# One load per attention-output unit and per output-weight piece, with rows ordered by head first and the value columns permuted

## The chip, the core and the metric

The kernel runs on one core of a Trainium2 chip. The metric is the device time of one execution in microseconds (us). Engines are named as the profile names them: PE (TensorE matmul), PEld (its weight load), DVE (VectorE), ACT (ScalarE), POOL (GpSimd) and SP (SyncE, which issues nearly all DMAs here). Before the change, the median of three runs is 849.85 us (848.42 to 851.2).

## What is computed

One layer: a normalized input goes through sliding-window attention (32 heads of width 20, window 256) and through a squared-relu MLP, and the attention is gated by the silu of the MLP.

```python
# S, D, F, H, Dh, W = 2048, 640, 1536, 32, 20, 256
xn = layernorm(x)
q, k, v = split_heads(xn @ wqkv)                  # 3 x 32 heads x 2048 x 20
scores = where(0 <= i - j < W, q @ k.T * Dh ** -0.5, -1e9)
s = concat_heads(softmax(scores) @ v) @ wo        # 640 x 640
r = relu(xn @ w1 + b1)
g = silu((r * r) @ w2 + b2)
out = x + s * g
```

All tensors are float32. The kernel splits an operand of a matmul into a rounded high part and a low rest, and takes three products (high by high, high by low, low by high).

## The kernel before

**Stages.** First (up to about 118 us) the input is normalized and transposed, the value weights `wv` are split, and the value products `vps` and the first query and key columns are made. Then follows one long loop of steps over head pairs and 128-row tiles; a step has score matmuls (`sps`, `stps`), the exponentials and, every few steps, a burst of value products (`ops`). Between them a filler puts matmuls of the remaining query/key columns (`qkps`), the MLP's first (`hps`) and second (`yps`) layer, and at the very end the output product (`wops`). PE's order is fixed when the program is built, and PE is in order.

**Order by a planner's clock.** Pieces that evacuate, split or fetch are put off by `later(wait, fn)`: they are emitted when a planned clock, advanced by the matmuls' planned costs, passes the due time. `BRING` is such a wait: the first unit's normalization, `turn_out(0, ...)`, comes `BRING` after its load was emitted.

**Value weights.** `load_w`/`wvr` bring five chunks of 128 rows of the value columns. `split_w` makes the high part on ACT (L188, `wv<-wvr`) and the rest on POOL (L189). The products `vps` (L233) for the first two row tiles take all high parts first (20 matmuls), then the five low parts, a chunk at a time.

**Attention output.** Each pair of heads, 512 rows of the sequence, and their sums of exponentials lie in a DRAM scratch `o_d[g]` as `[16 pairs, 128, 256]`: the 128 rows of a pair are four blocks of 32, by head and by parity of the row tile, of which 20 are the head's values and the next is its sum. A *unit* `u` (eight of them) is one parity of one `g`. `load(u)` brings it to `ob`, partitions `32 k + head`, chunk `c` holding value row `4 c + k` of the head: four DMAs of 32 partitions each (L1126), each with 5 runs of 256 numbers a partition. A fifth DMA (L1127) brings the inverted sums to `sums`. `turn_out(u, 0)` multiplies `ob` by `sums` on DVE (L1145, two pieces) and rounds it on ACT (L1146); `turn_out(u, 1)` makes the rests on DVE (L1149, two pieces). The output product (L627) of a unit contracts those 128 partitions, chunk by chunk, with five pieces of `wo` whose rows lie in the same order: each is four DMAs of 32 rows (L800) into `raw`, then a high part on ACT (L825) and a rest on DVE (L826).

**MLP output.** Each half row of `yps` (18 matmuls in each half of the array) is accumulated in one of three PSUM banks and evacuated by one DVE instruction, `ysb` (L1013). PE's next `yps` group in that bank waits for it.

**DMA queue.** SP issues in program order. Completion is counted on eight semaphores (`DMAHW0` to `DMAHW7` in the order of instructions) taken in turn, and a DMA waits until the one that had its semaphore before, eight earlier, is complete.

Of the kernel before, what the change touches and what calls it, by code (L numbers as in the profile page):

```python
# [19 lines left out]
H = 32  # L20
DH = 20
# [5 lines left out]
VW = DH + 1  # L27
# [7 lines left out]
MT = 256  # L35
# [14 lines left out]
SETTLE = 0.45  # L50
LEAD = 0.15
FETCH = 8.0
BRING = 8.0
SOON = 0.25
PATIENCE = 0.5

# [1 line left out]
def f32(ap):  # L58
    return ap.bitcast(F32)
# [3 lines left out]
def attn_mlp_kernel(ctx: ExitStack, tc, x, wqkv, wo, w1, b1, w2, b2, out):  # L63
    nc = tc.nc
# [25 lines left out]
    o_d = [dram.tile([NP, P, MT], F32, name=f"o_{g}") for g in range(NB)]  # L90
# [47 lines left out]
    with tc.tile_pool(name="ph1v", bufs=2) as p1v, tc.tile_pool(name="ph1", bufs=2) as p1, tc.tile_pool(name="ph1x", bufs=4) as p1b, tc.tile_pool(name="ph1w", bufs=1) as p1w, tc.tile_pool(name="ph1t", bufs=2, space=PSUM) as p1t:  # L138
# [9 lines left out]
        wv = [p1w.tile([P, KC, D], F32R, name=f"wv{p}") for p in range(2)]  # L148
# [119 lines left out]
        with tc.manual_schedule(engines={E_.PE, E_.Activation, E_.DVE, E_.Pool, E_.SP}):  # L268
# [15 lines left out]
            wjobs = []  # L284
# [6 lines left out]
            wvr = [wvt[c // 3][:, c % 3 * D:(c % 3 + 1) * D] for c in range(KC)]  # L291
            for c in range(KC):
                nc.sync.dma_start(wvr[c], wqkv[c * P:(c + 1) * P, 2 * D:3 * D])
                wjobs.append((wv[0][:, c, :], wv[1][:, c, :], wvr[c]))

            def root(t):
                nc.scalar.activation(rstd[:, t:t + 1], mv[:, t, 1:2], AF.Sqrt, bias=eps)
# [195 lines left out]
    def max_rows(p, g, tps):  # L493
        i = p % 2

        def one(j):
            r = slice(j * HP, (j + 1) * HP)
            nc.tensor.transpose(tps[:HP, j, 3 * P:3 * P + HP], mts[g % 2][r, :], ident[r, r])
        both(lambda: one(0), lambda: one(1), COST[P])

        def rest():
            row = at2.tile([8, P], F32, tag="row", bufs=1, name="row")
            mrow = at2.tile([8, 2, P], F32R, tag="mrow", bufs=1, name="mrow")
            nc.scalar.activation(row.rearrange("m (j n) -> m j n", j=2), tps[:8, :, 3 * P:3 * P + HP], AF.Copy, scale=-1.0)  # L504
            nc.scalar.activation(mrow[:, 0, :], row, AF.Copy)
            nc.gpsimd.tensor_sub(mrow[:, 1, :], row, f32(mrow[:, 0, :]))
            for a in range(2):
                nc.sync.dma_start(f32(qs[i])[KR + a:KR + a + HP + 1:HP, g * BT:(g + 1) * BT].rearrange("h (q n) -> h q n", q=4), f32(mrow)[:, a, :])
        return rest
# [3 lines left out]
    def pair_tile():  # L513
        return ptp.tile([P, 2, BT], F32, tag="st", name="stps")
# [25 lines left out]
    def burst_at(p, kb):  # L540
        return next((ts for ts in bursts(p) if ts[-1] == kb), None)
# [57 lines left out]
    def later(wait, fn):  # L599
        tasks.append((clock[0] + wait, len(tasks), fn))  # L600
# [177 lines left out]
    def subtract(tag, jobs):  # L778
        left = [len(jobs)]

        def put_off(k, job):
            def go():
                if item in lows:
                    lows.remove(item)
                    job()
                    left[0] -= 1
                    if not left[0]:
                        held[0] -= 1
            item = (tag, go)
            lows.append(item)  # L790
            later(1.9 + 0.7 * k, go)
        for k, job in enumerate(jobs):
            put_off(k, job)

    def piece(tag, src, go):
        def start():
            raw = wgt.tile([P, FHALF], F32, tag="wraw", bufs=RAW, name="raw")[:, :RAWN[tag[0]]]
            if isinstance(src, list):
                for k, rows in enumerate(src):
                    nc.sync.dma_start(raw[32 * k:32 * k + H], rows)  # L800
                return lambda tag: go(tag, raw)
            if len(src.shape) == 3:
                raw = raw.rearrange("p (c n) -> p c n", n=src.shape[-1])
            nc.sync.dma_start(raw, src)
            return lambda tag: go(tag, raw)
        queue.append((tag, start))
# [16 lines left out]
    def piece_pair(tag, hi, lo, src):  # L823
        def go(tag, raw):
            nc.scalar.activation(hi(), raw, AF.Copy)  # L825
            subtract(tag, [lambda: nc.vector.tensor_sub(lo(), raw, f32(hi()))])  # L826
        piece(tag, src, go)

    def lazy(make):
        got = []  # L830

        def get():
            if not got:
                got.append(make())
            return got[0]
        return get
# [42 lines left out]
    def filler():  # L879
# [53 lines left out]
        def late():  # L933
            j = lates[0]
            lates[0] += 1
            if j >= 3:
                load(0)
            if j >= 5:
                load(1)
            if j >= 7:  # L940
                load(2)

        for n, (hf, b) in enumerate(blocks):
# [6 lines left out]
            if n == last:  # L950
                wo_part = queue_wo()
                shut.add("o")
# [116 lines left out]
    rec_d = [dram.tile([2, H, MT], F32, name=f"rec_{g}") for g in range(NB)]  # L1069
# [47 lines left out]
    def load(u):  # L1117
        if u in ld or u >= 2 * NB or recs.get(u // 2, 0) is not None:
            return
        if u % 2 == 0:  # L1120
            obs[u // 2] = bigp.tile([P, KC * BT], F32, tag="big", name=f"ob_{u // 2}")
        ob = obs[u // 2][:, u % 2 * 2 * D:(u % 2 + 1) * 2 * D].rearrange("p (c n) -> p c n", c=KC)
        sums = at2.tile([P, MT if u // 2 % 3 == 0 else BT], F32, tag=("sums", "relu", "sq")[u // 2 % 3], name="sums")[:, :MT]
        rows = o_d[u // 2].rearrange("p (h r) n -> (p h) r n", h=2)[:, 32 * (u % 2):32 * (u % 2) + VW]
        for k in range(4):
            nc.sync.dma_start(ob[32 * k:32 * k + H], rows[:, k:DH:4])  # L1126
        nc.sync.dma_start(sums, rec_d[u // 2][u % 2].unsqueeze(0).to_broadcast([4, H, MT]))  # L1127
        ld[u] = (ob, sums)
        if not u:
            for part in range(2):  # L1130
                later(BRING + 2.0 * part, lambda part=part: turn_out(0, part))

    obs, oT, turned_out, shone = {}, {}, set(), set()

    def turn_out(u, part):
        if (u, part) in turned_out or u not in ld:
            return
        turned_out.add((u, part))
        ob, sums = ld[u]
        cuts = (slice(0, 2), slice(2, KC))  # L1140
        if not part:
            big = bigp.tile([P, KC * BT], F32R, tag="big", name=f"oT_{u}")
            oT[u] = big.rearrange("p (s c n) -> p s c n", s=2, c=KC)
            for cs in cuts:
                nc.vector.tensor_mul(ob[:, cs], ob[:, cs], sums.unsqueeze(1).to_broadcast([P, cs.stop - cs.start, MT]))  # L1145
                nc.scalar.activation(oT[u][:, 0, cs], ob[:, cs], AF.Copy)  # L1146
        else:
            for cs in cuts:
                nc.vector.tensor_sub(oT[u][:, 1, cs], ob[:, cs], f32(oT[u][:, 0, cs]))  # L1149
            if whole[0]:  # L1150
                silu(u)
# [9 lines left out]
    def queue_wo():  # L1161
        wob = lazy(lambda: [bigp.tile([P, KC * BT], F32R, tag="big", name=f"wo{j}") for j in range(2)])
        wo4 = lazy(lambda: [wgt.tile([P, FHALF], F32R, tag="wraw", bufs=RAW, name=f"wo4{w}")[:, :D] for w in "hl"])

        def wo_part(p, c):
            return wob()[p][:, c * D:(c + 1) * D] if c < 4 else wo4()[p]

        for c in range(KC):
            piece_pair("o", lambda c=c: wo_part(0, c), lambda c=c: wo_part(1, c), [wo.rearrange("(h d) n -> d h n", d=DH)[4 * c + k] for k in range(4)])
        return wo_part  # L1170

    def out_filler(wo_part):
# [71 lines left out]
    with tc.manual_schedule(engines={E_.PE, E_.Activation, E_.DVE, E_.Pool, E_.SP}):  # L1244
# [7 lines left out]
        for s in range(steps):  # L1252
# [8 lines left out]
            if a:  # L1261
                p, q = a
# [12 lines left out]
            rows = None  # L1275
# [4 lines left out]
            if s % 4 == 0 and 0 < s <= NP * NT:  # L1280
                rows = max_rows((s - 1) // NT, (s - 1) % NT // 4, stp[0] if b else pair_tile())
# [11 lines left out]
            r = e and burst_at(*e)  # L1293
# [41 lines left out]
```

## Time and profile before

| | before |
|---|---|
| median of three runs | 849.85 us |
| the profiled execution, its own time | 851.8 us |
| its span, first to last instruction | 849.7 us |
| mean granted TensorE clock | 0.995 |
| moved by DMA | 166.42 MB, mean 196 GB/s |
| `ob<-o` | 32 DMAs of 160 KB |
| `raw<-in_A_wo_dram` | 20 DMAs of 80 KB |
| `sums<-rec` | 8 DMAs of 128 KB |

So 2.1 us of the profiled execution lie outside its span. In the profile's timeline a row gives the start, the duration, the engine, the line, the instruction and its output and inputs; brackets hold the idle time of the engine before it and what ended it. The windows view gives the busy time of each engine in a stretch, with the instruction count in brackets, then the granted clock (PEclk, 1.00 is full), the busy share of the 16 DMA engines and the rate that they moved. The waits view sums who waited for whom: total, times, longest. A busy PE is not the same as a PE at its peak, because ends of matmuls are modelled.

### The profile page before, as it was taken

Reading aid. Unit: us, or ns where it says so; the run is one execution under the profiler, and the core shown is the slowest. Engines: PE = TensorE matmul, PEld = TensorE weight load, DVE = VectorE, ACT = ScalarE, POOL = GpSimd, SP = SyncE. Lnnn points to the kernel's source line nnn. Section 1 sums busy time; section 2 is a strip of 40 time slices with the busy share of each in tenths; the row PEclk is TensorE's granted clock in tenths of the full one; section 3 lists DMA queues with packets and bytes.
Section 4 is the critical chain, followed back from the end, with each engine's and each line's share of the span. In section 5 each row is a group of like instructions: output and inputs, shape, how many; then the busy total and the mean of one; then the engine's idle time right before and its main releaser. Section 6 shows DMA issues by size and latency. Waiting matters only on the chain.

```text
span 849.7 us, 25547 instructions
## 1 busy us (share of the span) xinstructions
PE 836.9 (98%) x10176; PEld 787.0 (93%) x10176; DVE 458.6 (54%) x1370; ACT 420.5 (49%) x792; POOL 329.9 (39%) x652
## 2 busy tenths in 40 slices
PE   8999999999999999999999999999999999989997
PEld 8999999988888999999999999899999999979997
DVE  7643126666577645455455476654455455345653
ACT  5232104555566754754754765745745736742321
POOL 5010002434334543553543644534533634532443
PEclk9999999999999999999999999999999999999999
DMA  7998488879989555364365264485285374376994
GB/s 245 284 389 336 161 207 259 256 249 273 300 268 302 128 182 156 84 200 132 78 214 166 77 179 136 128 266 154 63 269 135 110 223 120 102 171 180 274 231 150
DMA packets 94398, 166.42 MB, mean 196 GB/s; under 512 B 10952, under 2 KB 43848, under 8 KB 93256
## 3 DMA queue, kind: packets, MB, share of 16 engines
q1 hardware_dynamic: 94120, 164.64, 64.4%
q8 instruction: 80, 1.31, 0.7%
q14 instruction: 38, 0.31, 0.1%
q10 hardware_dynamic: 160, 0.16, 0.1%
HBM read 93.66 MB, written 70.52 MB: 193 GB/s over the span
## 4 chain that ended last, share of the span: by engine, by line
PE 87%; DMA 6%; DVE 2%; issue 2%; ACT 1%; SPq 1%; POOL 0%; DVEq 0%; ACTq 0%; POOLq 0%
PE yps L473 20%; PE hps L473 19%; PE qkps L473 14%; PE ops L561 10%; PE vps L233 8%; PE stps L523 5%; PE sps L483 4%; DMA ob<-o 4%; PE qkps L210 3%; PE wops L627 2%; DMA sums<-rec 1%; DMA yk<-y 1%; PE tps L177 1%; DMA o<-osb 1%; SPq L1126 0%
## 5 line engine op out<-in xcount | busy, mean ns | idle before, releaser
L491 DVE CUSTOM_DVE_ANT_0 junk<-sps,mask 128x384 bf16<-128x384 f32 (+2 forms) x512 | 272.1, 532 | 257.8 <-PE sps L483 86.8
L529 ACT ACTIVATE p<-stps 128x768 f32<-128x768 f32 (+2 forms) x256 | 197.4, 771 | 248.3 <-PE stps L523 203.0
L530 POOL TENSOR_SCALAR_AFFINE_SELECT p<-p 128x256 f32<-128x256 f32 x256 | 109.9, 429 | 326.1 <-ACT p L529 318.2
L473 PE MATMUL yps<-w,hh 64*128 64x320 f32 x1536 | 228.5, 312 | 4.2 <-DVE ysb L1013 3.4
L473 PE MATMUL hps<-xb,w 64*128 64x256 f32 (+1 forms) x2100 | 211.9, 304 | 0.0
L473 PEld LDWEIGHTS hps<-xb,w 64*128 64x128 f32 x2100 | 194.5, 187 | 3.8 <-issue 2.7
L473 PEld LDWEIGHTS yps<-w,hh 64*128 64x128 f32 x1536 | 187.0, 187 | 7.8 <-DVE ysb L1013 4.4
L473 PE MATMUL yps<-w,hl 64*128 64x320 f32 x768 | 177.8, 311 | 0.0
L483 PE MATMUL sps<-ks,qs 60*128 60x384 f32 (+2 forms) x512 | 131.5, 335 | 0.6 <-DVE mt L491 0.5
L523 PE MATMUL stps<-qs,ks 62*128 62x384 f32 (+2 forms) x512 | 126.3, 333 | 0.3 <-ACT row L504 0.2
L473 PEld LDWEIGHTS yps<-w,hl 64*128 64x128 f32 x768 | 120.4, 187 | 1.1 <-issue 1.0
L473 PE MATMUL qkps<-xT,wgkh 64*128 64x512 f32 x320 | 100.5, 394 | 0.0
L473 PE MATMUL qkps<-xT,wgqh 64*128 64x512 f32 x320 | 98.6, 392 | 0.0
L532 POOL TENSOR_SCALAR_AFFINE_SELECT p<-p 128x256 f32<-128x256 f32 x224 | 95.9, 428 | 0.0
L561 PE MATMUL ops<-p,vp 128*21 128x128 f32 (+1 forms) x2128 | 86.9, 311 | 0.0
L483 PEld LDWEIGHTS sps<-ks,qs 60*128 60x128 f32 x512 | 81.9, 185 | 4.4 <-DVE mt L491 2.2
L561 PEld LDWEIGHTS ops<-p,vp 128*21 128x21 f32 x2128 | 63.8, 100 | 21.2 <-issue 6.1
L523 PEld LDWEIGHTS stps<-qs,ks 62*128 62x128 f32 x512 | 80.7, 187 | 1.2 <-ACT row L504 0.6
L233 PE MATMUL vps<-wv,xT 128*128 128x320 f32 x480 | 71.5, 308 | 0.0
L233 PEld LDWEIGHTS vps<-wv,xT 128*128 128x128 f32 x480 | 70.5, 188 | 0.1
L983 POOL TENSOR_TENSOR hl<-sq,hh 128x512 fp32r<-128x512 f32 x48 | 62.2, 1295 | 16.4 <-ACT sq L982 16.2
L627 PE MATMUL wops<-wo,oT 128*128 128x320 f32 x384 | 62.2, 310 | 0.2 <-DVE res L1209 0.2
(104 smaller groups left out, 1160.1 us busy)
## 6 DMA issues: line engine op xcount, KB each, us to landing
ks<-k_d SPq DMA_DIRECT2D x64, 240.0 KB
qs<-q_d SPq DMA_DIRECT2D x64, 240.0 KB
xb<-xs SPq DMA_DIRECT2D x60, 256.0 KB
xs<-xT SPq DMA_DIRECT2D x8, 1280.0 KB
k_d<-shm SPq DMA_DIRECT2D x19, 512.0 KB
q_d<-shm SPq DMA_DIRECT2D x19, 512.0 KB
y<-ysb SPq DMA_DIRECT2D x28, 320.0 KB
o<-osb SPq DMA_DIRECT2D x64, 128.0 KB
```

What stands on the lines that cost most here:

```text
L210: nc.tensor.matmul(ps, wt[:, c, :], xT[part][b][:, c * BT + t0:c * BT + t0 + n], start=m == 1, stop=m == 3 * KC)
L233: nc.tensor.matmul(ps, xT[xp][b][:, c * BT + t * P: c * BT + (t + 1) * P], wv[wp][:, c, nh * HALF:(nh + 1) * HALF], start=first and m == 0 ...
L473: return nc.tensor.matmul(out, a[r], b_[r], skip_group_check=True, **kw)
L483: nc.tensor.matmul(ss[hh][:, :nk], qs[i][o, q * P:(q + 1) * P], ks[i][o, k0 * P:k0 * P + nk], start=True, stop=True)
L491: nc.vector.tensor_tensor_reduce(out=junk[:, :nk], in0=ss[hh][:, :nk], in1=mask[:, 3 * P - nk:], scale=1.0, scalar=-3.0e38, op0=ALU.add, o ...
L523: nc.tensor.matmul(tps[:, hh, :n], ks[i][o, kb * P:(kb + 1) * P], qs[i][o, kb * P:kb * P + n], start=True, stop=True)
L529: nc.scalar.activation(p32[:, :, :n], tps[:, :, :n], AF.Exp, scale=SCALE)
L530: nc.gpsimd.affine_select(p32[:, :, 0:P], p32[:, :, 0:P], pattern=[[0, 2], [1, P]], compare_op=ALU.is_ge, fill=0.0, base=0, channel_multip ...
L532: nc.gpsimd.affine_select(p32[:, :, 2 * P:], p32[:, :, 2 * P:], pattern=[[0, 2], [-1, P]], compare_op=ALU.is_gt, fill=0.0, base=0, channel ...
L561: nc.tensor.matmul(ot[r0:r0 + VW, c0:c0 + len(part), :], vps[p][:, kb // 4, kb % 4, hh, :], pt[:, hh, :].rearrange("p (t n) -> p t n", n=P ...
L627: nc.tensor.matmul(ps, a, b_, start=j == 0, stop=j == n - 1)
L983: nc.gpsimd.tensor_sub(hh[1][:, :BT], sq, f32(hh[0]))
```

## The change

The unit's rows are ordered by head first: `ob`'s partition is now `4 head + k`, and chunk `c` of it holds row `5 k + c` of the head in the scratch. So the five rows of a partition are one run of 1280 numbers, and the whole unit is one DMA of 128 partitions; `sums` is broadcast in the same order. For chunk `c`, partition `4 head + k` still to meet `wo` row `4 c + k` of the head, the 20 value columns of each head are permuted where `wv` is split: the split reads column `4 c + k` and writes column `5 k + c`. A `wo` piece is then the four rows `4 c` to `4 c + 3` of each head, one DMA of 128 partitions. `BRING` goes from 8 to 9.

```diff
-BRING = 8.0
+BRING = 9.0
...
-                wjobs.append((wv[0][:, c, :], wv[1][:, c, :], wvr[c]))
+                wjobs.append((*(w[:, c, :].rearrange("p (h k c) -> p h k c", h=H, k=4) for w in wv), wvr[c].rearrange("p (h c k) -> p h k c", h=H, k=4)))
...
-            if isinstance(src, list):
-                for k, rows in enumerate(src):
-                    nc.sync.dma_start(raw[32 * k:32 * k + H], rows)
+            if tag[0] == "o":
+                nc.sync.dma_start(raw, src)
                 return lambda tag: go(tag, raw)
...
-        rows = o_d[u // 2].rearrange("p (h r) n -> (p h) r n", h=2)[:, 32 * (u % 2):32 * (u % 2) + VW]
-        for k in range(4):
-            nc.sync.dma_start(ob[32 * k:32 * k + H], rows[:, k:DH:4])
-        nc.sync.dma_start(sums, rec_d[u // 2][u % 2].unsqueeze(0).to_broadcast([4, H, MT]))
+        rows = o_d[u // 2].rearrange("p (h r) n -> (p h) r n", h=2)[:, 32 * (u % 2):32 * (u % 2) + DH]
+        nc.sync.dma_start(ob.rearrange("p c n -> p (c n)"), rows.rearrange("h (k c) n -> h k (c n)", k=4))
+        nc.sync.dma_start(sums, rec_d[u // 2][u % 2].unsqueeze(1).to_broadcast([H, 4, MT]))
...
-            piece_pair("o", lambda c=c: wo_part(0, c), lambda c=c: wo_part(1, c), [wo.rearrange("(h d) n -> d h n", d=DH)[4 * c + k] for k in range(4)])
+            piece_pair("o", lambda c=c: wo_part(0, c), lambda c=c: wo_part(1, c), wo.rearrange("(h d) n -> h d n", d=DH)[:, 4 * c:4 * c + 4])
```

The order of PE's and POOL's instructions is the same in both programs. On DVE it differs in one place, at the first unit's normalization, just after the last `wo` piece. Before:

```order
L826 TENSOR_TENSOR wo4l<-raw,wo4h 128x640
L1084 RECIPROCAL rec<-rec 128x128
L1145 TENSOR_TENSOR ob_13901<-ob_13901,sums 128x512
L1145 TENSOR_TENSOR ob_13901<-ob_13901,sums 128x768
L1013 TENSOR_TENSOR ysb<-yps,yin 128x320
L1149 TENSOR_TENSOR oT_14055<-ob_13901,oT_14055 128x512
L1149 TENSOR_TENSOR oT_14055<-ob_13901,oT_14055 128x768
```

and now, at the same place of DVE's program:

```order
L825 TENSOR_TENSOR wo4l<-raw,wo4h 128x640
L1083 RECIPROCAL rec<-rec 128x128
L1012 TENSOR_TENSOR ysb<-yps,yin 128x320
L1143 TENSOR_TENSOR ob_13886<-ob_13886,sums 128x512
L1143 TENSOR_TENSOR ob_13886<-ob_13886,sums 128x768
L1147 TENSOR_TENSOR oT_14059<-ob_13886,oT_14059 128x512
L1147 TENSOR_TENSOR oT_14059<-ob_13886,oT_14059 128x768
```

The evacuation `ysb` has moved ahead of the two multiplications of `ob` (new lines are one or two lower in number). On ACT the last exponential, 128x2x128, likewise moves ahead of the first unit's two roundings.

On SP the queue before, from the load of the first units on (`o_85` to `o_88` are the four scratches `o_d`, `rec` the sums on their way through DVE):

```order
L1081 DMA rec<-o_86 64x1x128 x2
L1126 DMA ob_13901<-o_85 32x5x256 x4
L1127 DMA sums<-rec_1359 128x1x256
L1126 DMA ob_13901<-o_85 32x5x256 x4
L1127 DMA sums<-rec_1359 128x1x256
L930 DMA yin<-y_83 128x640
L1085 DMA rec_1360<-rec 128x128
L588 DMA o_87<-osb 128x256
L1081 DMA rec<-o_87 64x1x128 x2
L1126 DMA ob_14103<-o_86 32x5x256 x4
```

and now, from the same place:

```order
L1080 DMA rec<-o_86 64x1x128 x2
L1124 DMA ob_13886<-o_85 128x1x1280
L1125 DMA sums<-rec_1359 128x1x256
L1124 DMA ob_13886<-o_85 128x1x1280
L1125 DMA sums<-rec_1359 128x1x256
L929 DMA yin<-y_83 128x640
L1084 DMA rec_1360<-rec 128x128
L588 DMA o_87<-osb 128x256
L1080 DMA rec<-o_87 64x1x128 x2
L1124 DMA ob_14080<-o_86 128x1x1280
```

Where four loads stood, one stands; the order of the others is unchanged.

## The prediction

> **What bounds the kernel now.** I read the page's head first, then PE's waits, then the chain of waits around the longest one.
>
> ```profile
> span 849.7 us, 25547 instructions
> PE 836.9 (98%) x10176; PEld 787.0 (93%) x10176; DVE 458.6 (54%) x1370; ACT 420.5 (49%) x792; POOL 329.9 (39%) x652
> ```
>
> PE is busy for 836.9 of 849.7 us and its order does not change, so the time can fall only where PE waits or runs at a lower clock, and rise only where a new wait appears. PE's waits, and those of its weight loads, have one large entry:
>
> ```profile
> PE yps L473 <- DVE ysb L1013: 3.4, 1, 3.4
> PEld yps L473 <- DVE ysb L1013: 4.4, 4, 3.7
> ```
>
> One single wait of 3.7 us on the evacuation `ysb`. The chain of waits shows why it was late (start, duration, what):
>
> ```profile
> 748.49 2.05 PE yps L473 x28
> ...
> 756.50 4.22 DMA ob<-o
> 760.73 0.11 DVE ob L1145
> 761.32 0.95 DVE ob L1145
> 762.27 0.41 DVE ysb L1013
> 762.73 5.18 PE yps L473 x35
> ```
>
> and DVE's timeline at that place:
>
> ```profile
> 754.02 0.95 DVE L1084 RECIPROCAL rec<-rec 128x128 f32<-128x128 f32 x1
> 760.71 1.56 DVE L1145 TENSOR_TENSOR ob<-ob,sums 128x512 f32<-128x512 f32 x2 [5.74 <-DMA ob<-o]
> 762.19 0.48 DVE L1013 TENSOR_TENSOR ysb<-yps,yin 128x320 f32<-128x320 f32 x1
> 762.59 1.55 DVE L1149 TENSOR_TENSOR oT<-ob,oT 128x512 fp32r<-128x512 f32 x2
> 764.74 0.49 DVE L1013 TENSOR_TENSOR ysb<-yps,yin 128x320 f32<-128x320 f32 x1 [0.59 <-PE yps L473]
> ```
>
> DVE stood 5.74 us before the first `ob` multiplication, whose data was still landing. `ysb` is queued behind it, and PE wanted that PSUM bank. The wait has a second price, read in two windows:
>
> ```profile
> 757.00:763.00 6.00, 2.60 (x34) 2.34 (x32) 2.29 (x4) 1.33 (x2) 0.00 (x0) 0.91 0.97 187
> 763.00:775.00 12.00, 12.00 (x110) 11.21 (x111) 4.94 (x8) 4.81 (x9) 0.92 (x1) 0.76 0.59 151
> ```
>
> The third number from the end is the granted clock: 1.00 elsewhere, 0.91 and 0.76 here. PE came back slow: 35 matmuls took 5.18 us, 0.148 us each, against 2.05 us for 28, 0.073 each, just before the wait.
>
> **Part 1, the evacuation goes first.** In the new order `ysb` stands behind the reciprocal that ended at 754.97 and waits for its own matmuls and for a `yin` load, which SP issues ahead of the `ob` loads (749.07, below). It runs as soon as they end, before PE stops at about 759. This removes 3.7 us less one normal spacing, **3.6 us**, and the slow stretch, 5.18 - 35 x 0.073 = **2.6 us**. That doesn't hang on how fast the new load is, since `ob` no longer stands ahead of `ysb`.
>
> What is late next? After that wait PE begins only one more group with this bank rule; it goes on to the output product, which needs `oT`:
>
> ```profile
> 771.79 1.01 PE L627 MATMUL wops<-wo,oT 128*128 128x320 f32 x5
> 772.74 1.52 PE L561 MATMUL ops<-p,vp 128*21 128x128 f32 x40
> ```
>
> That start moves from 771.8 to 765.6. At the old landing, 760.7, multiplications and rests are done by 764.1 (the 762.59 row plus 1.55), so 1.5 us remain even with no faster load.
>
> **Part 2, the load itself.** SP's rows up to the first two units:
>
> ```profile
> 749.07 0.38 SPq L930 DMA_DIRECT2D yin<-y  x1
> ...
> 751.73 2.64 SPq L1126 DMA_DIRECT2D ob<-o  x4
> 754.41 0.58 SPq L1127 DMA_DIRECT2D sums<-rec  x1
> 755.03 1.91 SPq L1126 DMA_DIRECT2D ob<-o  x4
> ```
>
> Four issues become one, about 0.5 us instead of 1.9. The rate, from windows full of 32-partition `ob` loads and full of 128-partition loads of 2560 bytes a row (last number, GB/s):
>
> ```profile
> 754.00:759.00 5.00, 5.00 (x85) 4.61 (x78) 0.97 (x2) 0.87 (x2) 1.07 (x3) 1.00 1.04 216
> 789.00:793.00 4.00, 4.00 (x29) 4.00 (x29) 2.13 (x4) 0.47 (x1) 2.79 (x3) 1.00 1.05 408
> ```
>
> No row shows a 128-partition load with runs of 5120 bytes; between 216 and 408 I take 400, the row whose partitions are alike. A unit of 640 KB then takes 1.6 instead of 3.0 us. That matters at the end:
>
> ```profile
> 817.05 1.27 DVE L1209 TENSOR_TENSOR res<-wops,yk 128x320 f32<-128x320 f32 x3
> 822.48 1.56 DVE L1145 TENSOR_TENSOR ob<-ob,sums 128x512 f32<-128x512 f32 x2 [4.16 <-DMA ob<-o]
> ...
> 817.41 0.31 PE L627 MATMUL wops<-wo4h,oT 128*128 128x320 f32 x1
> 817.67 2.00 PE L627 MATMUL wops<-wo,oT 128*128 128x320 f32 x12
> ...
> 824.20 0.31 PE L627 MATMUL wops<-wo4h,oT 128*128 128x320 f32 x1
> 824.50 2.02 PE L627 MATMUL wops<-wo,oT 128*128 128x320 f32 x12
> ...
> 826.65 0.31 PE L627 MATMUL wops<-wo4h,oT 128*128 128x320 f32 x1
> 827.15 1.99 PE L627 MATMUL wops<-wo,oT 128*128 128x320 f32 x12 [0.19 <-DVE res L1209]
> ```
>
> DVE waits for loads there, and `wops` starts that normally follow at 0.147 us (1.76 for 12) come after 0.26, 0.30 and 0.50 us: 0.11 + 0.15 + 0.35 = **0.6 us** of PE. With six loads 1.4 us shorter each, 8.4 us of DMA time, I count all of it gone. The loads, stores and sums of the last stage follow PE by its evacuations, so they move 6.2 us earlier with it; the shorter loads are the cover for that. The single `wo` loads save SP issues under work that has slack (0 us), and the changed order of `sums` moves the same bytes (0 us).
>
> **Part 3, the permuted split at the start.** The POOL rests of `wv` now read `wvr` with a step of four numbers. ACT reads it so too.
>
> ```profile
> 15.27 7.68 POOL L189 TENSOR_TENSOR wv<-wvr,wv 128x640 fp32r<-128x640 f32 x5
> 20.27 8.96 PE L233 MATMUL vps<-wv,xT 128*128 128x320 f32 x60
> 15.29 1.99 ACT L188 ACTIVATE wv<-wvr 128x640 fp32r<-128x640 f32 x3
> 17.44 0.75 ACT L188 ACTIVATE wv<-wvr 128x640 fp32r<-128x640 f32 x1
> ```
>
> POOL goes through five rests of 1.54 us without a gap, to 22.95. PE starts at 20.27 and takes 0.149 us a matmul: after 20 high parts, at 23.25, it wants the five rests, the fifth at 23.85. Slack **0.9 us**: each rest may grow by 0.18 us for nothing, beyond that PE waits. ACT's last high part ends at 18.19 and is wanted at 20.27 + 8 x 0.149 = 21.46: 3.3 us over five pieces of 0.74, so it is covered unless they nearly double. The same values are made, so nothing later changes.
>
> No row shows a stepped read on POOL. The nearest are two fills of 64 numbers, with a step and without:
>
> ```profile
> L241 POOL MEMSET vt<- 128x64 f32 x8 | 1.8, 241 | 42.8 <-DMA v_d<-vt 42.8
> L104 POOL MEMSET mt<- 128x64 f32 x2 | 0.2, 151 | 0.0
> ```
>
> The stepped one costs 90 ns more, 1.4 ns a number; times 640 that is 0.9 us a rest. Ends: nothing, or 5 x 0.9 - 0.9 = 3.6 us of PE. The fill writes and the rest reads, so I take the middle, 0.54 us a rest: 2.7 - 0.9 = **1.8 us**, all on the fifth piece.
>
> [...]
>
> **Sum.** -3.6 - 2.6 - 0.6 + 1.8 = -5.0 us. The profiled execution, 851.8 us with 2.1 outside its span, would become 846.8. It lies 1.95 above the median, and on the median's scale the forecast is 849.85 - 5.0 = **844.8**. Its own range, from the two ends of the POOL price, is 843.0 to 846.6.
>
> **Rivals.**
>
> *The last stage gives half back.* PE's output product starts 6.2 us earlier, but the last loads don't. For: in the rows above DVE still waits 4.16 us for `ob`, so the loads there are just in time. Against: they get shorter, and what releases them moves too. At half of 6.2, 3.1 us come back: 847.9.
>
> *One load is no faster than four.* The change wouldn't do what it says: 216 GB/s stay, and the 0.6 us. Part 1 stands: 845.4.
>
> *The start takes it all.* The full 0.9 us a rest makes PE wait 1.3 us for the fourth piece and 2.3 for the fifth; if that also brings the half clock, as after 759, 2.6 us more. 849.85 - 6.8 + 6.2 = 849.2. For: the clock rows above. Against: two gaps, each shorter than that of 3.7. [...]
>
> *Slower.* One mechanism: POOL's stepped read doubles the rest to 3.2 us or more. Then 5 x 1.66 - 0.9 = 7.4 us of wait, a single gap above 3 us among it, and 2.6 of slow clock: 849.85 - 6.8 + 10.0 = 853.0. It decides from 3.1 us a rest on. Against: it needs nearly twice the upper end of the rows.
>
> **How the numbers follow.** Forecast 0.70; load no faster 0.08; last stage half back 0.07; start takes it all 0.09; slower 0.06. A difference of 0.3%, 2.5 us, is about what a measurement can tell from no change. So faster (below 847.3) gets the first two, 0.78; same the next two, 0.16; slower 0.06. The range reaches from 842.0 (no wait at the start, and a us of spread as the three runs show) to 848.3, which takes in the first three cases.
>
> **What would show it.** `ysb` at about 758, right behind the reciprocal, and no PE wait near 759; the granted clock 1.00 in 757 to 775; the first `wops` near 765.6 plus the wait at the start; `ob` loads near 400 GB/s, and PE's last 70 us without gaps; POOL's `wv` rests of about 2.1 us, and one gap of 1.8 in `vps` near 24. It is wrong if the rests take over 3 us, if the clock falls near 25, or if `wops` waits for DVE behind `ob`.

## The result and the profile after

The changed kernel takes 843.63 us (median of 4 runs, 843.34 to 843.87); the kernel before, on the same chip, 850.43 us. The ratio is 0.9923 (95% interval 0.9905 to 0.9942): 6.8 us less, between 4.9 and 8.1. The profiled execution took 843.45 us and its mean granted clock was 1.00. The forecast was 844.8, between 842.0 and 848.3: the time came out as predicted. The experiments below show that it did so largely for another reason than the one given.

First the page's head after the change:

```profile
span 841.7 us, 25475 instructions
PE 832.2 (99%) x10176; PEld 782.1 (93%) x10176; DVE 460.4 (55%) x1370; ACT 423.8 (50%) x792; POOL 333.5 (40%) x652
```

Of the 72 instructions fewer, 39 are DMA issues (24 of `ob`, 15 of `wo` pieces). PE has the same 10176 matmuls and is busy 4.7 us less, among it the slow stretch. PE's waits (total, times, longest) no longer have an entry for `ysb`, and that of its weight loads (PEld) is down from 4.4 to 0.7 us; one for the new split at the start has come:

```profile
PE vps L233 <- POOL wv L189: 0.8, 1, 0.8
PEld vps L233 <- POOL wv L189: 1.0, 1, 1.0
```

DVE's timeline at the place of the old wait, with the two windows that held the low clock:

```profile
756.96 0.49 DVE L1012 TENSOR_TENSOR ysb<-yps,yin 128x320 f32<-128x320 f32 x1 [2.56 <-POOL p L530]
757.37 1.76 DVE L1143 TENSOR_TENSOR ob<-ob,sums 128x512 f32<-128x512 f32 x2
```

```profile
757.00:763.00 6.00, 6.00 (x71) 6.00 (x70) 4.58 (x7) 4.51 (x6) 0.83 (x1) 1.00 0.44 152
763.00:775.00 12.00, 12.00 (x111) 11.22 (x111) 6.36 (x9) 3.00 (x5) 3.01 (x3) 1.00 0.68 226
```

`ysb` goes first, as ordered. The row below it says more: the `ob` multiplication has no bracket. Its data had landed already, at 757.4, where the kernel before still waited at 760.7. PE is busy in both windows throughout, at the full clock. The chain of waits, from there to the end:

```profile
756.63 8.27 PE yps L473 x85
764.90 0.93 PE wops L627 x5
765.83 1.45 PE ops L561 x40
767.28 69.87 PE wops L627 x475
```

The last 70 us are one gapless piece of PE. Before, the last piece of the chain was

```profile
827.15 17.90 PE wops L627 x120
```

with loads and DVE ahead of it. From the first output product (771.79 before, 764.90 now) to the last (845.05 and 837.15, the sums of those rows), 73.3 us became 72.3.

At the start, the tile view of `wv` after the change (durations min/median/max in ns, first and last start) and PE's row there:

```profile
L188 ACT ACTIVATE wv<-wvr x5: 1417/1437/1443, 12.5 to 18.6; 128x640 fp32r<-128x640 f32 x5
L189 POOL TENSOR_TENSOR wv<-wvr,wv x5: 1875/1923/1927, 14.0 to 21.5; 128x640 fp32r<-128x640 f32 x5
```

```profile
23.48 5.55 PE L233 MATMUL vps<-wv,xT 128*128 128x320 f32 x36 [0.79 <-POOL wv L189]
```

A POOL rest takes 1.92 us, 0.36 more than the 1.57 that the same view has for it before; an ACT high part takes 1.44 where it took 0.74.

### The profile page after: what moved, and what is told of

It reads as the page before. It is cut to its first block, busy times and chain, and to the rows that moved or that the text cites. A ratio compares the mean times of both kernels' runs of the same rounds, so it can differ in the third digit from the quotient of the medians.

```text
span 841.7 us, 25475 instructions
## 1 busy us (share of the span) xinstructions
PE 832.2 (99%) x10176; PEld 782.1 (93%) x10176; DVE 460.4 (55%) x1370; ACT 423.8 (50%) x792; POOL 333.5 (40%) x652
## 4 chain that ended last, share of the span: by engine, by line
PE 94%; issue 1%; POOL 1%; ACT 1%; DVE 1%; DMA 1%; SPq 0%; DVEq 0%; POOLq 0%
PE yps L473 21%; PE hps L473 20%; PE qkps L473 14%; PE ops L561 10%; PE wops L627 8%; PE vps L233 8%; PE stps L523 5%; PE sps L483 4%; PE qkps L210 2%; POOL wv L189 1%; PE tps L177 1%; DMA raw<-in_A_wqkv_dram 1%; DVE junk L491 0%; ACT p L529 0%; ACT relu L977 0%
## 5 line engine op out<-in xcount | busy, mean ns | idle before, releaser
L473 PE MATMUL yps<-w,hh 64*128 64x320 f32 x1536 | 226.1, 309 | 0.8 <-ACT relu L977 0.8
L473 PEld LDWEIGHTS yps<-w,hh 64*128 64x128 f32 x1536 | 184.2, 185 | 4.1 <-ACT relu L977 1.6
L473 PE MATMUL yps<-w,hl 64*128 64x320 f32 x768 | 175.3, 308 | 0.0
L523 PE MATMUL stps<-qs,ks 62*128 62x384 f32 (+2 forms) x512 | 128.0, 333 | 0.2 <-ACT row L504 0.2
L473 PEld LDWEIGHTS yps<-w,hl 64*128 64x128 f32 x768 | 117.8, 185 | 1.1 <-issue 1.0
```

Source lines behind the costliest of these rows:

```text
L473: return nc.tensor.matmul(out, a[r], b_[r], skip_group_check=True, **kw)
L523: nc.tensor.matmul(tps[:, hh, :n], ks[i][o, kb * P:(kb + 1) * P], qs[i][o, kb * P:kb * P + n], start=True, stop=True)
```

## The experiments

The question is which of the change's parts carries the gain: the order of DVE's work (`BRING`), the single load, its long runs, the weight loads, the permutation, or the order of partitions, with the `sums` load that follows it. Each kernel was timed in several rounds against the kernel before on the same chip. Medians are given with that of the kernel before on that chip, because the latter moves between chips (848.2 to 850.4).

### The parts undone one at a time

The changed kernel with the old order of DVE's work:

```diff
-BRING = 9.0
+BRING = 8.0
```

> The changed kernel with BRING at 8 again: DVE has the two ob multiplications ahead of ysb, as before the change, but the unit is one load. In the changed kernel's trace the multiplications began at 757.37, right behind ysb, so the load had landed by then. If what blocks ysb is only the landing of ob, a load that lands by about 757 lets ysb run by about 759 and PE doesn't stop, or for well under 1 us: 843.6 us, at most 844.6, granted clock 1.00 throughout. Rival, that the order on DVE is the cause by itself: PE stops near 759 as before and the clock falls, some 6 us of the gain are lost: about 849.5.

Measured: 844.06 us (before 849.51; ratio 0.9934, 0.9919 to 0.9948), and PE does not wait for `ysb`. The changed kernel again on that chip:

> The changed kernel again, on the same chip as the three others and for comparison with them: 843.6 us by every theory, granted clock 1.00 throughout, POOL's wv rests at 1.92 us, PE's wait for them 0.8 to 1.0 us.

Measured: 844.03 us (ratio 0.9934, 0.992 to 0.9949). So the new order isn't needed in this kernel. The other way round, the kernel before with the new order alone:

```diff
-BRING = 8.0
+BRING = 9.0
```

> The kernel before with BRING at 9 alone: ysb ahead of ob on DVE, four loads a unit, the value weights split in order. If the wait of ysb behind ob cost 3.6 us and the slow clock after it 2.6, this gives back 6.2 of 850.4: 844.2 us, with the small gaps in the last stage (0.6 to 1.0 us) still there and no wait on the value weights at the start. Rival, that the loads' speed is what the gain comes from: the first wops then waits for oT behind a load that lands at 760.7, or the last stage gives the time back: 847 to 850 us.

Measured: 849.83 us (ratio 1.0004, 0.9992 to 1.0015). The order alone gains **nothing**. Yet it does what the prediction said: in the chain, `wops` starts at 764.01, 7.8 us earlier than before, with no wait near 759. Not all of the 7.8 is its doing, since this execution was ahead from the start: the first `vps` began at 19.03 where the profiled execution before has 20.27.

```profile
19.03 8.96 PE L233 MATMUL vps<-wv,xT 128*128 128x320 f32 x60
```

PE's order is the same in both, so the traces can be laid side by side matmul by matmul: just ahead of the old wait this one is 1.5 us ahead (the same `yps` matmul at 756.08 and 757.56), so the wait and the slow clock were worth 6.4, close to the 6.2 foretold. The time comes back in the last stage. The waits view, PE's and DVE's rows there, and the chain:

```profile
PE wops L627 <- DVE res L1209: 4.4, 3, 3.8
```

```profile
802.66 2.63 PE L627 MATMUL wops<-wo,oT 128*128 128x320 f32 x12 [3.81 <-DVE res L1209]
800.64 1.56 DVE L1145 TENSOR_TENSOR ob<-ob,sums 128x512 f32<-128x512 f32 x2 [7.87 <-DMA out_dram<-res]
```

```profile
764.01 0.93 PE wops L627 x5
...
784.25 7.58 DMA yk<-y
791.83 0.02 issue
791.85 8.62 DMA sums<-rec
...
800.85 6.84 DMA ob<-o
807.68 0.02 issue
807.70 9.02 DMA ob<-o
...
825.28 17.84 PE wops L627 x120
```

It is the same pattern as the wait that was removed: DVE stands before an `ob` multiplication, an evacuation (`res`) is queued behind it, and PE wants the bank. The bracket of the row at 800.64 names a store (`out_dram`), but in the chain the load of `sums` lands just before it, at 791.85 + 8.62 = 800.47. The chain is made of transfers one behind the other. The output product now lasts from 764.01 to 843.12, 79.1 us instead of 73.3: 5.9 of the 6.4 us gained are given back. Most of the 1.9 us between the two spans (849.7 and 847.8) is the earlier start; the medians show no gain.

Last, the changed kernel without the permuted columns; the `wo` rows are gathered in the matching order instead, still by one load a piece:

```diff
-wjobs.append((*(w[:, c, :].rearrange("p (h k c) -> p h k c", h=H, k=4) for w in wv), wvr[c].rearrange("p (h c k) -> p h k c", h=H, k=4)))
+wjobs.append((wv[0][:, c, :], wv[1][:, c, :], wvr[c]))
...
-piece_pair("o", ..., wo.rearrange("(h d) n -> h d n", d=DH)[:, 4 * c:4 * c + 4])
+piece_pair("o", ..., wo.rearrange("(h k c) n -> h k c n", h=H, k=4)[:, :, c])
```

> The changed kernel with the value columns left in order, and the wo pieces taken as rows 5k+c of each head (one load of 128 rows, none next to another): the same result without the stepped split. If PE's wait of 0.8 to 1.0 us on POOL near 23 us is carried to the end, 0.9 us less than the changed kernel: 842.7 us, POOL's rests of wv back at 1.55 us, ACT's high parts at 0.74, and no wait of vps for POOL. Rival, that the start's wait is taken up by slack later on, or that wo rows apart land later than PE wants them: 843.6 us or more.

Measured: 842.49 us (ratio 0.9918, 0.9901 to 0.9935), 1.5 less than the changed kernel on that chip. The permutation isn't needed and costs. Most of its price shows at one place in the chain, the transposes behind the first 60 `vps`. With the permutation (the changed kernel on this chip), and without:

```profile
29.56 2.18 PE tps L177 x20
```

```profile
28.29 2.18 PE tps L177 x20
```

They start 1.3 us later with it, though `vps` itself starts at nearly the same time, 19.39 with it and 19.32 without.

### Number of loads and length of runs

These four start from the kernel without the permutation. Four loads of `ob` in place of one, to partitions `4 head + k`, still in runs of 5 KB:

```diff
-nc.sync.dma_start(ob.rearrange("p c n -> p (c n)"), rows.rearrange("h (k c) n -> h k (c n)", k=4))
+for k in range(4):
+    nc.sync.dma_start(ob.rearrange("(h k) c n -> k h (c n)", k=4)[k], rows.rearrange("h (k c) n -> k h (c n)", k=4)[k])
```

> As the run without the permutation (842.5 us), but a unit in four loads again: load k goes to the partitions 4h+k, 32 of them spread over all 128, in runs of 5 KB. It changes the number of loads alone. If the number counts (each load takes one of eight semaphores, so that fewer bytes are under way, and 0.45 us of SP), the last stage falls behind: 845 us or more, with gaps in wops. If the partitions or the run length count, the loads still move 330 GB/s or more and it stays at 842.5.

Measured: 842.53 us (before 849.57; ratio 0.9918, 0.9905 to 0.9931). The same four loads in runs of 1 KB, with `wo` ordered to match:

```diff
+for k in range(4):
+    nc.sync.dma_start(ob.rearrange("(h k) c n -> k h c n", k=4)[k], rows[:, k:DH:4])
```

> Four loads a unit to the partitions 4h+k, spread over all 128, but in runs of 1 KB: chunk c of partition 4h+k is value row 4c+k again, and no column is permuted. If neighbouring partitions halve the rate, this one is fast: 330 GB/s and 842.5 us. If short runs do, about 200 GB/s and 847 to 850 us.

Measured: 842.59 us (0.992, 0.9907 to 0.9933). Four loads for each `wo` piece:

```diff
-nc.sync.dma_start(raw, src)
+for k in range(4):
+    nc.sync.dma_start(raw.rearrange("(h k) n -> k h n", k=4)[k], src.rearrange("h k n -> k h n")[k])
```

> As the run without the permutation, a unit in one load, but each wo piece in four loads of 32 rows again. If the wo loads are under other work, as forecast, no difference: 842.5 us. If SP's twelve and eight issues in the steps before delay what is queued behind them, 0.4 us or more is lost between 740 and 750: 843 us.

Measured: 842.75 us (0.9921, 0.9908 to 0.9934). None of the three differs from 842.49 by more than 0.3 us. One load in place of four, and long runs in place of short ones, gain nothing that shows here, where `sums` is loaded in its new form. Then the old partitions, 32 neighbouring ones a load, with long runs:

```diff
+for k in range(4):
+    nc.sync.dma_start(ob[32 * k:32 * k + H].rearrange("p c n -> p (c n)"), rows[:, 5 * k:5 * k + 5].rearrange("h c n -> h (c n)"))
-nc.sync.dma_start(sums, rec_d[u // 2][u % 2].unsqueeze(1).to_broadcast([H, 4, MT]))
+nc.sync.dma_start(sums, rec_d[u // 2][u % 2].unsqueeze(0).to_broadcast([4, H, MT]))
...
+piece_pair("o", ..., wo.rearrange("(h k c) n -> k h c n", h=H, k=4)[:, :, c])
```

> Again four loads a unit in runs of 5 KB, but load k goes to the consecutive partitions 32k to 32k+31, as before the change; the sums and the wo rows follow that order, each wo piece in one load. If 32 neighbouring partitions are what halves the rate, the loads move some 200 GB/s and the last stage stalls PE as with BRING 9 alone: 847 to 850 us. If the run length counts, 330 GB/s and 842.5 us.

Measured: **851.18** us (1.0032, 1.0018 to 1.0047). The whole gain is gone, and PE waits in the last stage again:

```profile
PE wops L627 <- DVE res L1208: 5.3, 4, 3.3
```

But this kernel changes two things beside where `ob` lands. With partitions `32 k + head`, `sums` must be filled by a source whose outermost dimension is the four-fold repeat, `[4, 32, 256]`, and the single `wo` load has the form `[4, 32, 640]`. The chain runs through the latter too: it holds such a `wo` load of 8.74 us, and the first `ob` load is issued only behind it, at 754.45, where the kernel with four loads to partitions `4 head + k` issues it at 748.93.

```profile
743.87 8.74 DMA raw<-in_A_wo_dram
```

The kernel before loads `wo` in another way, so for its loss two theories were left: the 32 neighbouring partitions of the `ob` loads (theory P), or the form of the `sums` load (theory S).

### The sums load alone

To separate them, the inverted sums are stored four times over in DRAM. The load of `sums` then is 128 plain rows, and `ob` can keep the loads that it had. (The store of the inverted sums becomes two DMAs instead of one.) By theory P that leaves the new order's 849.83 us as it is. On the kernel before:

```diff
-BRING = 8.0
+BRING = 9.0
...
-rec_d = [dram.tile([2, H, MT], F32, name=f"rec_{g}") for g in range(NB)]
+rec_d = [dram.tile([2, 4, H, MT], F32, name=f"rec_{g}") for g in range(NB)]
...
-nc.sync.dma_start(rec_d[g].rearrange("a h (j n) -> (a h j) n", n=P), recs[g])
+for par in range(2):
+    nc.sync.dma_start(rec_d[g][par].rearrange("k h (j n) -> (h j) k n", n=P), recs[g][64 * par:64 * (par + 1)].unsqueeze(1).to_broadcast([64, 4, P]))
...
-nc.sync.dma_start(sums, rec_d[u // 2][u % 2].unsqueeze(0).to_broadcast([4, H, MT]))
+nc.sync.dma_start(sums, rec_d[u // 2][u % 2].rearrange("k h n -> (k h) n"))
```

> The kernel before with two edits: the outputs' multiplications queued behind the projection of the other half (the order that alone gained nothing, 849.8), and the inverted sums stored four times over in DRAM, so that the load of sums is 128 plain rows instead of a four-fold repeat of 32. The unit's outputs still come by four loads, each to 32 neighbouring partitions, in runs of 1 KB. [...] Theory S (the gain comes from the load of sums, whose source had only four outer steps): 842.5 to 843.5, no wait in the last stage, as in the kernel without the permutation (842.49).

Measured: **843.03** us (before 848.83; ratio 0.9931, 0.9918 to 0.9943). With the `ob` loads of before, four of them, each in short runs to 32 neighbouring partitions, the gain is there. The kernel of 851.18 without its two other changes, as an edit of the one just timed:

```diff
-nc.sync.dma_start(ob[32 * k:32 * k + H], rows[:, k:DH:4])
+nc.sync.dma_start(ob[32 * k:32 * k + H].rearrange("p c n -> p (c n)"), rows[:, 5 * k:5 * k + 5].rearrange("h c n -> h (c n)"))
...
-..., [wo.rearrange("(h d) n -> d h n", d=DH)[4 * c + k] for k in range(4)])
+..., [wo.rearrange("(h d) n -> d h n", d=DH)[5 * k + c] for k in range(4)])
```

> As the run with the sums stored four times, but each of the four output loads takes five neighbouring rows of each head, so that its runs are 5 KB, still to 32 neighbouring partitions (the weight's rows are ordered to match, in four loads a piece). It is the earlier run with neighbouring partitions (851.18) without its two other changes, the repeated source of sums and the single load of a weight piece. Theory P: 848 to 850. Theory S: 842.5 to 843.5. A third outcome, e10 slow and this one fast, would say that it takes short runs and neighbouring partitions together.

Measured: 843.02 us (0.9935, 0.9921 to 0.9948). And the reference:

> The changed kernel without the permuted value columns once more, as the reference on this chip: 842.5, between 842.2 and 843.0, by both theories.

Measured: 842.61 us (0.9932, 0.9919 to 0.9944). The theory of the partitions fell in both runs; the form of the `sums` load stands. The extra store can't be the cause, since the changed kernel and those with four loads to partitions `4 head + k` are as fast without it. What it does is seen by putting the issue of `sums` beside the multiplication that waited for it. From the kernel before with the new order alone, units 0, 3 and 5, SP's queue first, then DVE, with unit 7's multiplication as the last row:

```profile
752.24 0.58 SPq L1127 DMA_DIRECT2D sums<-rec  x1
781.38 0.55 SPq L1127 DMA_DIRECT2D sums<-rec  x1
802.35 0.54 SPq L1127 DMA_DIRECT2D sums<-rec  x1
...
758.61 1.56 DVE L1145 TENSOR_TENSOR ob<-ob,sums 128x512 f32<-128x512 f32 x2 [2.05 <-DMA sums<-rec]
787.27 1.56 DVE L1145 TENSOR_TENSOR ob<-ob,sums 128x512 f32<-128x512 f32 x2 [3.29 <-DMA sums<-rec]
810.71 1.56 DVE L1145 TENSOR_TENSOR ob<-ob,sums 128x512 f32<-128x512 f32 x2 [4.10 <-DMA sums<-rec]
828.48 1.56 DVE L1145 TENSOR_TENSOR ob<-ob,sums 128x512 f32<-128x512 f32 x2 [2.55 <-DMA out_dram<-res]
```

and the same units with the sums stored four times:

```profile
753.11 0.44 SPq L1128 DMA_DIRECT2D sums<-rec  x1
780.09 0.44 SPq L1128 DMA_DIRECT2D sums<-rec  x1
798.45 0.43 SPq L1128 DMA_DIRECT2D sums<-rec  x1
...
757.39 1.56 DVE L1146 TENSOR_TENSOR ob<-ob,sums 128x512 f32<-128x512 f32 x2 [0.72 <-DMA sums<-rec]
784.75 1.70 DVE L1146 TENSOR_TENSOR ob<-ob,sums 128x512 f32<-128x512 f32 x2 [0.67 <-DMA sums<-rec]
804.13 1.56 DVE L1146 TENSOR_TENSOR ob<-ob,sums 128x512 f32<-128x512 f32 x2 [2.45 <-DMA sums<-rec]
819.20 2.24 DVE L1146 TENSOR_TENSOR ob<-ob,sums 128x512 f32<-128x512 f32 x2
```

From issue to multiplication 6.4, 5.9 and 8.4 us became 4.3, 4.7 and 5.7: 2.1, 1.2 and 2.7 less, **2.0 us a unit** on average. Over all eight units, from the issue of `sums` to the last update of its semaphore in the trace, 7.2 us became 5.4 on average, 1.8 less. `sums` is the last load of a unit, so DVE starts that much sooner. And it sets a cycle: four units apart, from 787.27 to 828.48 in DVE's rows, the first kernel takes 10.3 us a unit, while PE needs 69.87 / 8 = 8.7. The second takes 8.6 (784.75 to 819.20), which keeps up with PE, so PE doesn't wait in this stage:

```profile
766.49 69.87 PE wops L627 x475
```

Last, that edit alone, with the old order of DVE's work (`BRING` 8):

> The kernel before with one edit: the inverted sums stored four times over in DRAM, so that the load of sums is 128 plain rows. The order of the multiplications (queued ahead of the projection of the other half), the four output loads in runs of 1 KB, the weight pieces and the value columns are those of the kernel before. Theory: the source of sums carries the gain alone; 842.7 to 844.5 (843.0 with the other order, and up to 1.5 more for a wait near 759 that may stay). Rival: the order and the sums are both needed; 846 to 849, with TensorE waiting several us for ysb near 759.

Measured: **844.19** us (before 848.24; ratio 0.9956, 0.9943 to 0.9969; nine of the ten runs lie between 843.6 and 845.7, the tenth at 849.08). One load's form, with nothing else of the change, gives 4.1 us by the medians, 2.6 to 4.8 by the interval. What is left of the old wait:

```profile
756.79 1.56 DVE L1146 TENSOR_TENSOR ob<-ob,sums 128x512 f32<-128x512 f32 x2 [3.44 <-DMA sums<-rec]
758.80 0.56 PE L473 MATMUL yps<-w,hh 64*128 64x320 f32 x4 [1.28 <-DVE ysb L1013]
```

and the two windows that held the low clock:

```profile
757.00:763.00 6.00, 4.72 (x52) 4.45 (x49) 3.94 (x7) 4.39 (x6) 0.92 (x1) 1.00 0.81 199
763.00:775.00 12.00, 12.00 (x112) 11.22 (x111) 5.94 (x10) 3.00 (x5) 2.58 (x3) 1.00 0.78 235
```

PE waits 1.28 us instead of 3.4, and the clock stays at 1.00 behind it. So once `sums` comes early, the order of DVE's work is worth about a us here (the spans are 842.1 and 841.0, on two chips), and nothing in the changed kernel. The reason isn't a quicker load: with the old order the first multiplication begins there at 756.89, no earlier than here, but PE comes to the place 1.9 us later (the same `yps` matmul at 757.66 and 755.74), behind the permuted split and a later first `vps`. Whether the old order would cost anything without the permutation wasn't run.

## Why the prediction came out right, step by step

**Part 1, the order: the step that failed.** The prediction gave it 6.2 us, more than the whole net gain of 5.0, with the words "That doesn't hang on how fast the new load is". The mechanism was seen where it was foretold: in the run with the order alone the wait and the slow clock near 759 are gone. But the gain does hang on the loads: with the old ones 849.83 against 849.51. What is late next was worked out only at the first output product. For the eight units behind it the prediction took it that the loads "follow PE by its evacuations, so they move 6.2 us earlier with it", and they don't: with the order alone PE comes to the output product 7.8 us earlier, but the last unit's multiplication only 2.8 (828.48 where the kernel before has 831.32). The loads take 10.3 us a unit against PE's 8.7. Before the change the stall near 759 hid most of that: the units came at 9.9 us there too (791.76 to 831.32 in DVE's rows), but PE began the stage late enough for only 0.6 us of gaps to be left.

**The term set at zero.** "The changed order of `sums` moves the same bytes (0 us)" is the line that should have carried the gain: 4.1 us alone, 5.8 with the order (843.03 against 848.83). The bytes are the same; the form of the source isn't. What differs shows in the trace's semaphore record. The old source `[4, 32, 256]` has four as its outermost dimension, and each of the eight `sums` loads of the kernel before updated its semaphore five times, once about 1.0 us after its issue and four times at its landing, 4.8 us or more after it. The new one, `[32, 4, 256]`, has 32, and the 128 plain rows have 128; each of these loads, in the changed kernel and with the sums stored four times, updated it sixteen times, all at its landing. The same five updates stand for the slow `wo` load above, whose form is `[4, 32, 640]`. So the two forms land in four and in sixteen parts.

An estimate of what that is worth, from these counts and the mean packet of the kernel before: the queue line

```profile
q1 hardware_dynamic: 94120, 164.64, 64.4%
```

gives 0.644 x 16 x 849.7 / 94120 = 93 ns a packet. If the parts move side by side and the packets of one part one after another, 128 packets of 1 KB are 32 in each of four parts or 8 in each of sixteen, so 3.0 or 0.7 us, 2.2 less, beside the 2.0 measured at three units and 1.8 over all eight. (The 1 KB packets alone, from 750 to 835 us of that trace, took 77 ns on average, which makes it 1.8.) How the parts move is not told by the trace, so the estimate rests on that assumption; that the form decides is shown.

**Part 2, the load: a cover that wasn't the one.** The 0.6 us of gaps in the last stage are gone (73.3 to 72.3 us from first to last output product, 1.0 less). The single faster load isn't why: with four loads in short runs, and the new `sums`, the stage is gapless too. The rate did rise, though less than to the 400 taken: 345 GB/s in the window full of `ob` loads, which before had 216. The second row is the same window in the kernel with four loads and the sums stored four times: 210 GB/s, and no gap behind it.

```profile
754.00:759.00 5.00, 5.00 (x82) 4.79 (x72) 2.44 (x4) 1.89 (x4) 1.40 (x3) 1.00 0.96 345
754.00:759.00 5.00, 5.00 (x74) 5.00 (x72) 2.10 (x4) 1.92 (x5) 0.81 (x2) 1.00 1.13 210
```

The sentence "the shorter loads are the cover for that" holds if `sums` is read for `ob`. The zero for the `wo` loads held (842.75 beside 842.49).

**Part 3, the permuted split: right mechanism, size too large.** The growth of a POOL rest was taken as 0.54 us and measured 0.36. By the prediction's own slack that is 5 x 0.36 - 0.9 = 0.9 us, and the waits are 0.8 and 1.0 us. Undoing it gave back 1.5 us, beside the 1.8 foretold; 1.2 of that (1.27, less the 0.07 by which `vps` starts earlier without it) is the place above, and where the rest comes from is open. ACT's high parts were "covered unless they nearly double": they did (0.74 to 1.44 us), and no wait of PE for them shows, only one of 0.2 us of its weight loads.

**The rivals.** "The last stage gives half back" named the place and the reason (loads just in time), and it is what happens to the order alone, only nearly in full (5.9 of 6.4). In the changed kernel it doesn't come to pass, because of `sums`. "One load is no faster than four: 845.4" was wrongly priced for the same reason as Part 1. The two at the start ask for a rest of 2.4 us or more, and it took 1.92; the clock stayed at 1.00.

So the number was right by luck, because two errors of the same size met: 6.2 us were credited to an edit that gives nothing by itself, and none to the edit that gives 4.1 alone and 5.8 with it.

**The best version** is the changed kernel without the permutation: 842.49 and 842.61 us on two chips, where the kernel before took 849.51 and 848.83. It keeps the head-first order of `ob`, the single loads and the new form of `sums`.

## What to carry to other kernels

Look at the outermost dimension of every DMA's source as well as its bytes and runs: here a 128 KB load that repeats 32 rows four times landed 1.6 us later with the repeat outermost than with the heads outermost (7.3 us against 5.7 from issue to landing, mean of eight units, in the kernels before and after), and as the last load of its unit it held a whole stage. Where a removed wait lets a stage start earlier, compare the period of that stage's loads with the period of the engine they feed before counting the gain. And undo the parts of a change one at a time even when the forecast came true.

## What the runs showed of the hardware that was not expected

- ScalarE reading 640 float32 a row in groups of five at a step of four numbers, and writing them in order, took 1.44 us instead of 0.74, nearly twice; POOL's two-input operation with one input read in that way took 1.92 instead of 1.57, 23% more.
- Behind a PE wait of 3.4 us the granted clock was 0.76 in the next 12 us; behind one of 1.28 us, in the same place, it was 1.00.
- One load in runs of 5 KB moved `ob` at 345 GB/s, four loads of 1 KB runs at 216 or 210, and the time of this kernel hardly depends on it (842.61 and 843.03 us on one chip, with `sums` early): what PE waited for was the small load queued last.
- Two loads whose source had four as its outermost dimension were slow: `sums` (128 KB, 5.6 to 9.7 us from issue to landing, where the changed kernel has 4.3 to 6.8) and, in the kernel of 851.18, `wo` (320 KB, 7.1 to 12.8 us, where the single `wo` load of the changed kernel took 3.3 to 4.6).
